# The second product of the last two blocks as seven products of half width

## The chip, the cores and the metric

The kernel runs on one core of a Trainium2 chip. A core has a matmul engine (PE; its weight loads are listed apart as PEld), a vector engine (VectorE, DVE in the profile), a scalar engine (ScalarE, ACT), GpSimd (POOL) and SyncE (SP); the last two issue transfers here, each on a queue of its own, and 16 transfer engines serve both. The metric is the device time of one execution in microseconds.

## The reference

A transformer block over 2048 tokens of 512 numbers: an adaptive layer norm (scale and shift from a condition row `c`), linear attention, a second adaptive layer norm, and a two-layer network with 1792 hidden columns. The change touches the last part only:

```python
h = layernorm(x) * (1 + cb) + sb
h = einsum("bsd,df->bsf", h, w1) + b1
act = mish(h)
x = x + gb * einsum("bsf,fd->bsd", act, w2)      # the second product
```

All of it is float32. D is 512, S is 2048, F is 1792.

## The kernel before

The tokens go in four blocks of 512, and the hidden columns in 14 tiles of 128 (`f`), or seven pairs of tiles (`g`). Every large product is made in "rounded" float32, whose matmul takes one pass: an operand is split into a high and a low half (`split`: ScalarE copies the high half, VectorE subtracts it for the low one), and `mm3` (lines 65 to 69) makes three matmuls, high by high, high by low and low by high. A matmul streams up to 512 columns past 128 x 128 weights, and each matmul loads its weights anew.

The first product takes two blocks together. `pair_unit(c0, g)` makes seven products instead of eight from 2 x 2 parts: two blocks of tokens by two halves of the 512 inputs by two tiles of w1 (a Strassen scheme; `rows(g)` makes the sums of w1's parts and splits them, `columns` those of the tokens). Each of the seven is six matmuls of 512 columns. VectorE adds the parts up from PSUM (`add`, line 848), ScalarE applies Mish (`mish`, `mish_b`). For the first of the two blocks the halves of the activations are made at once; those of the second wait in `ub` until `prep_a` splits them.

The second product is made block by block: `d_unit(b, f)` multiplies the four token tiles of tile `f` by w2's tile `f`, 512 columns, into four banks of PSUM (`oacc`), 12 matmuls; after the 14th tile VectorE adds the residual (line 831) and SP stores the block.

w2 is scaled by `gb` and split once (`w2_job`), and its halves are written to DRAM (`w2d`). They are used by block 0 at once; for blocks 1, 2 and 3 `w2_again` reads them back, 28 transfers of 256 KB a block on POOL's queue, four tiles ahead in block 1 and block 3. w1 is read and prepared by `rows` twice, once for blocks 0 and 1, once for 2 and 3.

The order of the work is written by hand: the engines' queues run in the order of the program. `spawn` puts a side job (a generator) on a list and `tick` takes each of them one step further, so that a step lands between two groups of matmuls. On-chip memory is 101 slots of 128 x 512 float32 (`sb`); a transfer into a slot waits for the last reader of what it held. The order from block 0 on is:

- for each pair `g`: `pair_unit(0, g)`, and, trailing by one or two tiles, block 0's `d_unit`; side jobs prepare w2 and the next w1, and the norms of blocks 2 and 3 (`norm_tile`).
- `second(1, prepare)`: block 1's 14 `d_unit`; side jobs transpose and prepare the tokens of blocks 2 and 3 and the first two w1 pairs again.
- for each pair: `pair_unit(2, g)`, trailed by block 2's `d_unit`.
- `second(3, end)`: block 3's 14 `d_unit`.

Of the kernel before, what the change touches and what calls it, by code (L numbers as in the profile page):

```python
# [8 lines left out]
F32 = mybir.dt.float32  # L9
F32R = mybir.dt.float32r  # L10
# [3 lines left out]
P = 128  # L14
# [11 lines left out]
def block_kernel(ctx: ExitStack, tc: tile.TileContext, x, wqkv, wo, w1, b1t, w2, c, wmodt, out):  # L26
# [23 lines left out]
    def spawn(gen):  # L50
        fresh.append(gen)

    def tick():

        running.extend(fresh)
        fresh.clear()
        for g in list(running):
            if next(g, "end") == "end":
                running.remove(g)

    def run(gen):
        for _ in gen:
            pass

    def mm3(o, st, mv, start, stop):

        pe.matmul(o, st[0], mv[0], start=start, stop=False)  # L67
        pe.matmul(o, st[0], mv[1], start=False, stop=False)  # L68
        pe.matmul(o, st[1], mv[0], start=False, stop=stop)  # L69

    def split(name, t, keep, key, lo_engine=dve, hi_engine=act):

        hi, lo = sb(f"{name}h", F32R, t.shape), sb(f"{name}l", F32R, t.shape)
        if hi_engine is act:
            act.activation(hi, t, AF.Copy)
        else:
            hi_engine.tensor_copy(hi, t)
        if lo_engine is dve:
            yield
        lo_engine.tensor_tensor(lo, t, f32(hi), op=ALU.subtract)  # L80
        keep[key] = hi, lo
# [412 lines left out]
            dve.tensor_scalar(zs[k], zbc, mc[:, k:k + 1], 1.0, op0=ALU.mult, op1=ALU.mult)  # L494


    w2s, w2d, op_a = {}, {}, {}

    w2r = {}

# [4 lines left out]
    def w2_job(f, wait=2):  # L505
        if f not in w2r:
            load_w2(f)
            for _ in range(wait):
                yield
        t = w2r[f]  # L510
        dve.tensor_tensor(t, t, bc["gb"], op=ALU.mult)
        yield
        yield from split(f"w2_{f}", t, w2s, f)
        yield
        for i in range(2):
            w2d[f, i] = drp.tile([P, D], F32R, name=f"w2d_{f}_{i}")
            pool.dma_start(w2d[f, i], w2s[f][i])

    def w2_again(f):

        w2s[f] = [sb(f"w2b_{f}_{i}", F32R) for i in range(2)]
        for i in range(2):
            pool.dma_start(w2s[f][i], w2d[f, i])  # L523

    def rows(g, wait):

        r = [sb(f"w1p_{g}_{i}", F32, (P, 4, P)) for i in range(2)]
        for i in range(2):
            f = 2 * g + i
            sp.dma_start(r[i], w1[:, P * f:P * (f + 1)].rearrange("(k p) f -> p k f", p=P))  # L530
        for _ in range(wait):
            yield
        a11, a12, a21, a22 = [r[i][:, 2 * k:2 * k + 2, :] for i in range(2) for k in range(2)]
        s12, s34 = [sb(f"s{n}_{g}", F32, (P, 4, P)) for n in (12, 34)]
        s1, s2, s3, s4 = s12[:, 0:2, :], s12[:, 2:4, :], s34[:, 0:2, :], s34[:, 2:4, :]
        dve.tensor_tensor(s1, a21, a22, op=ALU.add)
        dve.tensor_tensor(s2, s1, a11, op=ALU.subtract)
        dve.tensor_tensor(s3, a11, a21, op=ALU.subtract)
        dve.tensor_tensor(s4, a12, s2, op=ALU.subtract)
        yield  # L540
        keep, todo = {}, []
        for name, v, parts in (("a1", r[0], ("a11", "a12")), ("s12", s12, ("s1", "s2")), ("s34", s34, ("s3", "s4")),
                               ("a22", a22, ("a22",))):
            half = split(f"{name}_{g}", v, keep, name)
            next(half)
            todo.append((name, half, parts))
            if len(todo) == 2:
                yield
                for name, half, parts in todo:
                    run(half)  # L550
                    for i, part in enumerate(parts):
                        op_a[g, part] = [h[:, 2 * i:2 * i + 2, :] for h in keep[name]]
                todo = []

    early_rows = [rows(g, 1) for g in range(2)]

# [77 lines left out]
    def o_post(p, b, t):  # L634
        r = xt["r", b, t]
        dve.tensor_tensor(r, p, r, op=ALU.add)  # L636
        if b >= 2:
            yield
            d = x1d[b, t] = drp.tile([P, D], F32, name=f"x1d_{b}_{t}")
            pool.dma_start(d, r)  # L640

    def o_unit(b, t, tag="acc"):
        p = ps(tag, f"o_{b}_{t}")
# [50 lines left out]
    def load_back(key, src, b, t):  # L694
        v = xt[key, b, t] = sb(f"{key}b_{b}_{t}")
        sp.dma_start(v, src.pop((b, t)))
# [112 lines left out]
            tick()  # L809


    ag = {}

    def mish(p, b, f):
        u = sb(f"u_{b}_{f}")
# [5 lines left out]
    def d_unit(b, f):  # L821
        if f == 0:
            for t in range(4):
                oacc[t] = ps("acc", f"oacc_{b}_{t}")
        for t in range(4):
            ts = slice(P * t, P * (t + 1))
            mm3(oacc[t], [a[:, ts] for a in ag[b, f]], w2s[f], f == 0, f == NF - 1)
            if f == NF - 1:
                v = xt["r", b, t]
                r0 = 512 * b + P * t  # L830
                dve.tensor_tensor(v, oacc[t], v, op=ALU.add)  # L831
                sp.dma_start(out[r0:r0 + P, :], v)
# [61 lines left out]
    def ahead(b, u):  # L894

        if 0 <= u - NF + 4 < NF:
            w2_again(u - NF + 4)
        if 0 <= u - NF + 3 < NF:
            spawn(prep_a(b, u - NF + 3))

    G = NF // 2
    order = [(b, c + h) for c in range(2) for h in (0, 2) for b in (2, 3)]
# [1 line left out]
    def prepare(f):  # L904

        if f in (1, 3, 5, 7):
            for _ in range(2):
                transpose_f(*order.pop(0), "h")
        if f in (4, 8):
            spawn(columns(2, f // 4 - 1, ()))  # L910
        if f in (6, 10):
            spawn(rows((f - 6) // 4, 2))

    def end(f):
        if 4 <= f < 8:
            load_back("r", x1d, 3, f - 4)


    begun = {}
# [7 lines left out]
    def trail(f):  # L927
        if tiles:
            spawn(tiles.pop(0))
        d_unit(0, f)  # L930
        ahead(1, f)
        tick()

    for g in range(G + 1):
        if g < G:
            for f in (2 * g, 2 * g + 1) if g else ():
                spawn(w2_job(f))
            if g == 0:
                spawn(rows(2, 3))
            pair_unit(0, g, begun.pop(g, None))  # L940
            if 0 < g < G - 2:
                spawn(rows(g + 2, 2))
            if g == G - 1:
                for n in range(8):
                    load_back("n", nd, 2 + n // 4, n % 4)
        for f in ((0,), (1,))[g] if g < 2 else (2 * g - 2, 2 * g - 1):
            trail(f)
    second(1, prepare)
    for g in range(G + 1):
        if g < G:  # L950
            w2_again(2 * g)
            w2_again(2 * g + 1)
            pair_unit(2, g)
            if g + 2 < G:
                spawn(rows(g + 2, 2))
            if g == G - 2:
                for t in range(4):
                    load_back("r", x1d, 2, t)
        for f in (2 * g - 2, 2 * g - 1):
# [37 lines left out]
```

## Time and profile before

| | |
|---|---|
| median of 3 runs | 504.34 us (504.11 to 505.1) |
| profiled execution, its own time | 504.41 us |
| its span | 502.7 us |
| granted clock of the matmul engine | 1.00 |
| transfers | 77.29 MB, 60.83 MB read from DRAM, 15.99 MB written |

The profile is one execution. Its times are from the start of the span; the 1.7 us between the span and the time lie around it. In the timeline a row has the start, the length, the engine, the line of the kernel, the operation and the tiles (out<-in, buffer numbers left out), the partitions and elements, and the count where equal ones follow each other. In the table by stretches each engine has its busy time and its count of instructions, then come the granted clock, the mean busy share of the transfer engines and the rate. Matmuls overlap: the length of one holds its drain, and the step from one start to the next is what a matmul costs in a row of them.

### The profile page before, as it was taken

The page shows a single profiled execution, that of the slowest core. Times are in us where ns is not written, and L with a number is a line of the kernel's source. Part 1 is how long each engine was busy: PE and PEld are TensorE (multiplying, and loading weights), DVE is VectorE, ACT ScalarE, POOL GpSimd, SP SyncE. Part 2 cuts the span into 40 slices and gives each one's busy share as a digit, 9 for nine tenths or more (in the row PEclk, how much of TensorE's full clock was granted, in tenths as well). Part 3 has the DMA queues.
Part 4 walks back from the last instruction along what each step waited for, and adds up shares of the span by engine and source line. Part 5 has one row for each costly group of instructions (what it writes and reads, how often), then busy time and mean ns, then how long its engine had stood idle before and what let it go on. Part 6 is the DMA issues. An engine that isn't in the chain of part 4 may idle for free.

```text
span 502.7 us, 6896 instructions
## 1 busy us (share of the span) xinstructions
PE 495.2 (99%) x2396; PEld 405.5 (81%) x2396; DVE 360.1 (72%) x707; ACT 257.9 (51%) x463; POOL 113.7 (23%) x204
## 2 busy tenths in 40 slices
PE   7999999999999999999999999999999999999996
PEld 6778888878778888888888888888888888888885
DVE  6889785889997979987987776359885656745302
ACT  6766574523351978745777764366253355445000
POOL 4471000100212423000233345421110111470000
PEclk9999999999999999999999999999999999999999
DMA  8721503471554316352555498982941445596002
GB/s 310 277 83 44 166 22 106 145 254 53 141 131 135 84 43 193 106 167 65 185 172 188 152 316 257 349 237 74 261 134 45 124 126 157 154 359 221 31 1 83
DMA packets 52233, 77.29 MB, mean 154 GB/s; under 512 B 5805, under 2 KB 20277, under 8 KB 52198
## 3 DMA queue, kind: packets, MB, share of 16 engines
q0 software_dynamic: 19600, 37.45, 25.7%
q1 hardware_dynamic: 32452, 39.14, 24.9%
q8 instruction: 19, 0.31, 0.2%
q10 hardware_dynamic: 146, 0.26, 0.1%
q14 instruction: 16, 0.13, 0.1%
HBM read 60.83 MB, written 15.99 MB: 153 GB/s over the span
## 4 chain that ended last, share of the span: by engine, by line
PE 95%; DVE 2%; DMA 1%; ACT 1%; POOL 0%; issue 0%; ACTq 0%
PE oacc L67 10%; PE oacc L68 10%; PE oacc L69 10%; PE p_s L67 5%; PE p_s L68 5%; PE p_s L69 5%; PE p_a L67 4%; PE p_a L68 4%; PE p_a L69 4%; PE o L67 3%; PE pq L67 3%; PE o L69 3%; PE o L68 3%; PE pq L69 3%; PE pq L68 3%; PE gacc L68 3%
## 5 line engine op out<-in xcount | busy, mean ns | idle before, releaser
L523 POOL DMA_DIRECT2D w2b<-w2d x84 | 44.9, 538 | 101.7 <-PE p_a L69 27.3
L839 ACT ACTIVATE ub<-c,b1c 128x512 f32<-128x512 f32 x28 | 19.2, 719 | 57.0 <-DVE c L848 53.3
L848 DVE TENSOR_TENSOR u<-p_s,u 128x512 f32<-128x512 f32 x28 | 19.3, 691 | 35.2 <-PE p_s L69 25.6
L831 DVE TENSOR_TENSOR rb<-oacc,rb 128x512 f32<-128x512 f32 x8 | 5.5, 691 | 32.9 <-PE oacc L69 32.9
L848 DVE TENSOR_TENSOR u<-p_a,u 128x512 f32<-128x512 f32 x26 | 17.5, 687 | 7.6 <-PE p_a L69 6.9
L189 POOL TENSOR_TENSOR rs_n<-rs_n,half 128x1 f32<-128x1 f32 x16 | 9.8, 617 | 54.8 <-DVE rs_n L215 44.9
L705 ACT ACTIVATE hf_n<-tp_n,mc 128x512 f32<-128x512 f32 x16 | 11.7, 770 | 18.9 <-PE tp_n L703 18.9
L816 ACT ACTIVATE u<-u,b1c 128x512 f32<-128x512 f32 x26 | 18.5, 712 | 2.6 <-DVE u L848 2.6
L241 ACT ACTIVATE e_q<-pq 128x512 f32<-128x512 f32 x16 | 9.4, 588 | 20.0 <-PE pq L69 20.0
L848 DVE TENSOR_TENSOR c<-p_s,u 128x512 f32<-128x512 f32 x28 | 17.9, 681 | 2.3 <-PE p_s L69 2.3
L865 ACT ACTIVATE u<-p_a 128x512 f32<-128x512 f32 x12 | 7.1, 588 | 18.7 <-PE p_a L69 18.7
L241 ACT ACTIVATE e_k<-pk 128x512 f32<-128x512 f32 x16 | 9.4, 591 | 13.3 <-PE pk L69 13.1
L189 POOL TENSOR_TENSOR rs_x<-rs_x,half 128x1 f32<-128x1 f32 (+1 forms) x10 | 7.1, 716 | 33.0 <-DVE rs_x L184 32.2
L243 DVE TENSOR_SCALAR e_k<-e_k 128x512 f32<-128x512 f32 x16 | 6.8, 424 | 10.2 <-ACT e_k L241 10.0
L198 ACT ACTIVATE x<-x,nb_x,rs_x 128x512 f32<-128x512 f32 x15 | 11.5, 806 | 4.4 <-DVE nb_x L193 3.3
L624 DVE TENSOR_TENSOR q<-q,rd 128x512 f32<-128x512 f32 x16 | 10.5, 686 | 3.8 <-DMA rd<-rden_d 3.8
L612 POOL DMA_DIRECT2D rden_d<-rden x3 | 2.2, 738 | 43.4 <-DVE rden L610 43.4
L198 ACT ACTIVATE r<-r,nb_n,rs_n 128x512 f32<-128x512 f32 x8 | 6.5, 809 | 10.1 <-DVE nb_n L219 9.3
L244 DVE SCALAR_TENSOR_TENSOR ku<-pk,e_k 128x512 f32<-128x512 f32 x16 | 11.1, 692 | 0.7
L244 DVE SCALAR_TENSOR_TENSOR q<-pq,e_q 128x512 f32<-128x512 f32 x16 | 11.1, 691 | 0.7
L636 DVE TENSOR_TENSOR r<-o,r 128x512 f32<-128x512 f32 x16 | 10.8, 677 | 1.1 <-PE o L69 1.1
L180 DVE BATCH_NORM_STATS2 st_x<-x 128x6 f32<-128x512 f32 x13 | 8.9, 682 | 3.0 <-DMA x<-in_x_dram 3.0
(1118 smaller groups left out, 1751.5 us busy)
## 6 DMA issues: line engine op xcount, KB each, us to landing
w2b<-w2d POOLq DMA_DIRECT2D x84, 256.0 KB, 5.0
w1p<-in_w_dram SPq DMA_DIRECT2D x28, 256.0 KB, 3.5
wm<-in_wmodt_dram SPq DMA_DIRECT2D x24, 256.0 KB, 5.0
r<-in_x_dram SPq DMA_DIRECT2D x16, 256.0 KB, 2.7
x<-in_x_dram SPq DMA_DIRECT2D x15, 256.0 KB, 4.8
w2r<-in_w_dram SPq DMA_DIRECT2D x14, 256.0 KB, 2.7
rd<-rden_d POOLq DMA_DIRECT2D x12, 256.0 KB, 5.3
wr<-in_wqkv_dram SPq DMA_DIRECT2D x8, 256.0 KB, 4.8
```

The lines of the kernel that those rows point to most:

```text
L67: pe.matmul(o, st[0], mv[0], start=start, stop=False)
L68: pe.matmul(o, st[0], mv[1], start=False, stop=False)
L69: pe.matmul(o, st[1], mv[0], start=False, stop=stop)
L189: pool.tensor_tensor(y, y, half[:, lo:hi], op=ALU.pow)
L198: act.activation(dst, t, AF.Identity, bias=nb[key, b][:, j:j + 1], scale=rs[key, b][:, j:j + 1])
L241: act.activation(e, p, AF.Exp)
L244: dve.scalar_tensor_tensor(dst, p, 0.0, e, op0=ALU.max, op1=ALU.add)
L523: pool.dma_start(w2s[f][i], w2d[f, i])
L705: act.activation(hf[b, j], p, AF.Identity, bias=mc[:, 12 + j:13 + j], scale=mc[:, 16 + j:17 + j])
L816: act.activation(u, p, AF.Mish, bias=b1c[:, f:f + 1])
L839: act.activation(u, p, AF.Mish, bias=b1c[:, f:f + 1])
L848: dve.tensor_tensor(out, p, u, op=ALU.add)
```

## The change

Block 0 and the first product stay as they are. Five things change.

1. The second product of blocks 2 and 3 is made for both together, as seven products for each pair `g` (two blocks, two tiles of w2, two halves of 256 output columns). m1 and m2 use w2's parts as they are (`e_unit`, made between the `pair_unit`s), m4, m6, m7, m5 and m3 come after the last pair, each over all seven pairs. `seventh` makes one product for one pair: four token tiles, `mm3` on 256 columns, two token tiles to a bank.
2. The sums of w2's parts are made during block 1's second product (`w2_sums`), from the scaled w2, which `w2_job` now also writes to DRAM unsplit for pairs 0 to 4 (`w2f`), and are written to DRAM (`w2t`) for five of the pairs and kept for pairs 3 and 4. `load_wt` and `load_wb` read them and w2's own parts back.
3. The sums of the activations are made by `left_sums` and split, and `finish` adds the seven products up to the four quarters of the output, which are stored by quarter.
4. w1's operands, made once by `rows`, are written to DRAM for pairs 0 to 4 (`store_rows`, SP's queue) and read back for blocks 2 and 3 (`load_rows`, POOL's queue); those of pairs 5 and 6 stay in their slots, and the second round of pairs starts with them.
5. Block 1's second product takes the tiles of w2 in the order 10 to 13, 0 to 9, and the first four are still in their slots from block 0.

The core of it:

```diff
+    KEPT, SUMS_KEPT = 5, (3, 4)
 def w2_job(f, wait=2):
 ...
-            w2d[f, i] = drp.tile([P, D], F32R, name=f"w2d_{f}_{i}")
-            pool.dma_start(w2d[f, i], w2s[f][i])
+            pool.dma_start(w2d[g, i][:, n, :], w2s[f][i])
+        if g < KEPT:
+            pool.dma_start(w2f[g][:, n, :], t)
+    W2_AT = {0: 6, 1: 5, 2: 0, 3: 1, 6: 2, 10: 3, 12: 4}
+    def w2_sums(g):
+        if g < KEPT:
+            r = [sb(f"w2p_{g}_{i}") for i in range(2)]
+            for i in range(2):
+                sp.dma_start(r[i], w2f[g][:, i, :])
+        else:
+            r = [w2r[2 * g + i] for i in range(2)]
+        yield
+        yield
+        h = D // 2
+        b11, b12, b21, b22 = [v[:, c:c + h] for v in r for c in (0, h)]
+        ta, tb = [sb(f"t{n}_{g}") for n in (12, 34)]
+        t1, t2, t3, t4 = ta[:, 0:h], ta[:, h:D], tb[:, 0:h], tb[:, h:D]
+        for d, u, v in (t1, b12, b11), (t2, b22, t1), (t3, b22, b12), (t4, t2, b21):
+            dve.tensor_tensor(d, u, v, op=ALU.subtract)
+        yield
+        keep = {}
+        both = [split(f"t{i}_{g}", v, keep, i) for i, v in enumerate((ta, tb))]
 ...
+        d = w2t[g] = drp.tile([P, 2, 4, h], F32, name=f"w2t_{g}")
+        for i in range(2):
+            for n in range(2):
+                sp.dma_start(d[:, n, 2 * i:2 * i + 2, :], f32(keep[i][n]).rearrange("p (t c) -> p t c", t=2))
 ...
+    last_first = [*range(2 * KEPT, NF), *range(2 * KEPT)]
     def second(b, side):
-        for f in range(NF):
-            side(f)
-            ahead(b, f + NF)
+        for n, f in enumerate(last_first):
+            side(n)
+            ahead(b, n + NF)
             tick()
-            d_unit(b, f)
+            d_unit(b, f, n)
 ...
+    def seventh(name, tag, left, right, n, last):
+        if n == 0:
+            banks[name] = [ps(tag, f"{name}_{i}") for i in range(2)]
+        for t in range(4):
+            h = t % 2
+            mm3(banks[name][t // 2][:, D // 2 * h:D // 2 * (h + 1)], [a[:, P * t:P * (t + 1)] for a in left], right,
+                n == 0 and h == 0, n == last and h == 1)
+    def e_unit(n):
+        g = pairs[n]
+        for c, name in enumerate(("m1", "m2")):
+            seventh(name, "acc", ag[L, 2 * g + c], [w[:, c, :] for w in wb[g]], n, G - 1)
+    def left_sums(g):
+        a11, a12, a21, a22 = ua[2 * g], ua[2 * g + 1], ub[2 * g], ub[2 * g + 1]
+        yield from split(f"l4_{g}", a22, left, ("m4", g))
+        dve.tensor_tensor(a22, a21, a22, op=ALU.add)
+        dve.tensor_tensor(a21, a11, a21, op=ALU.subtract)
+        yield
+        dve.tensor_tensor(a11, a22, a11, op=ALU.subtract)
+        dve.tensor_tensor(a12, a12, a11, op=ALU.subtract)
 ...
-    for g in range(G + 1):
-        if g < G:
-            w2_again(2 * g)
-            w2_again(2 * g + 1)
-            pair_unit(2, g)
-            if g + 2 < G:
-                spawn(rows(g + 2, 2))
 ...
-            if f >= 0:
-                d_unit(2, f)
-            ahead(3, f)
-            tick()
-    second(3, end)
+    pairs = [5, 6, 0, 1, 2, 3, 4]
+    for n, g in enumerate(pairs):
+        if n < 5:
+            if n:
+                load_rows(n)
+            if n:
+                load_wb(pairs[n + 1])
 ...
+        pair_unit(L, g)
+        if n < 4:
+            spawn(left_trail(g))
+        if n:
+            e_unit(n - 1)
+            tick()
+    names = ["m4", "m6", "m7", "m5", "m3"]
+    units = [(name, n) for name in names for n in range(G)]
+    ahead_of = units[4:]
 ...
+    for k, (name, n) in enumerate(units[:4 * G]):
+        for _ in range(2 if k in (6, 10, 14, 18) else 1):
+            if ahead_of:
+                nm, m = ahead_of.pop(0)
+                spawn(left_prep(nm, pairs[m]))
 ...
+        seventh(name, tags[name], left.pop((name, pairs[n])), wt.pop((name, pairs[n])), n, G - 1)
+        if n == G - 1:
+            spawn(finish(name))
+        tick()
+        if k == 1:
+            e_unit(G - 1)
+            spawn(finish("m2"))
+            tick()
+    last = [ps("acc", f"m3_{t}") for t in range(4)]
+    for t in range(4):
+        p = last[t][:, 0:D // 2]
+        for n, g in enumerate(pairs):
+            mm3(p, [a[:, P * t:P * (t + 1)] for a in left["m3", g]], wt["m3", g], n == 0, n == G - 1)
+        tick()
+        v = rq[0, 1, t // 2][:, t % 2, :]
+        dve.tensor_tensor(v, v, p, op=ALU.add)
+        store(0, 1, t // 2, t % 2, t % 2 + 1)
```

`load_rows(0)` and the first two `load_wb` stand at the last two tiles of block 1's second product.

More of the change, by code (lines that the diff above doesn't have):

```diff
@@ L553, in rows, with store_rows, load_rows @@
                 todo = []
+    op_rows, rows_d = {}, {}
+    def store_rows(g):
+        for name, halves in op_rows.pop(g).items():
+            for i, h in enumerate(halves):
+                rows_d[g, name, i] = drp.tile(list(h.shape), F32, name=f"rd_{g}_{name}_{i}")
+                sp.dma_start(rows_d[g, name, i], f32(h))
+    def load_rows(g):
+        for name, parts in ("a1", ("a11", "a12")), ("s12", ("s1", "s2")), ("s34", ("s3", "s4")), ("a22", ("a22",)):
+            halves = []
+            for i in range(2):
+                d = rows_d.pop((g, name, i))
+                halves.append(sb(f"{name}b_{g}_{i}", F32R, d.shape))
+                pool.dma_start(halves[i], d)
+            for i, part in enumerate(parts):
+                op_a[g, part] = [h[:, 2 * i:2 * i + 2, :] for h in halves]
     early_rows = [rows(g, 1) for g in range(2)]
@@ L910, in prepare @@
             spawn(columns(2, f // 4 - 1, ()))
[L911 to L916, printed above, removed]
+        if f in W2_AT:
+            spawn(w2_sums(W2_AT[f]))
+        if f == NF - 2:
+            load_rows(0)
+            load_wb(5)
+        if f == NF - 1:
+            load_wb(6)
     begun = {}
@@ new lines, in left_trail, with left_prep, add_r, finish @@
+    def left_trail(g):
+        yield
+        yield
+        yield from left_sums(g)
+    def left_prep(name, g):
+        return left_sums(g) if name == "m4" else split(f"l_{name}_{g}", sums_of[g][name], left, (name, g))
+    def add_r(n, c, i, v, op=ALU.add):
+        dve.tensor_tensor(rq[n, c, i], rq[n, c, i], v, op=op)
+    def finish(name):
+        for i in range(2):
+            p = bank(name, i)
+            if name == "m2":
+                U[i] = sb(f"U_{i}", F32, (P, 2, D // 2))
+                act.activation(U[i], bank("m1", i), AF.Copy)
+                add_r(0, 0, i, bank("m1", i))
+                add_r(0, 0, i, p)
+                store(0, 0, i)
+            if name == "m4":
+                add_r(1, 0, i, p, ALU.subtract)
+            if name == "m6":
+                dve.tensor_tensor(U[i], U[i], p, op=ALU.add)
+                add_r(0, 1, i, U[i])
+            if name == "m7":
+                dve.tensor_tensor(U[i], U[i], p, op=ALU.add)
+                add_r(1, 0, i, U[i])
+                store(1, 0, i)
+                add_r(1, 1, i, U[i])
+            if name == "m5":
+                add_r(0, 1, i, p)
+                add_r(1, 1, i, p)
+                store(1, 1, i)
+            yield
@@ new lines, in block_kernel, with load_wt @@
+    wt, SUM = {}, {"m5": 0, "m6": 1, "m7": 2, "m4": 3}
+    def load_wt(name, g):
+        h = D // 2
+        if name != "m3" and g in SUMS_KEPT:
+            n = SUM[name]
+            wt[name, g] = [w2k[g][n // 2][i][:, h * (n % 2):h * (n % 2 + 1)] for i in range(2)]
+            return
+        v = sb(f"wt_{name}_{g}", F32R, (P, 2, h))
+        wt[name, g] = [v[:, i, :] for i in range(2)]
+        if name == "m3":
+            for i in range(2):
+                pool.dma_start(v[:, i, :], w2d[g, i][:, 1, D // 2:D])
+        else:
+            pool.dma_start(v, w2t[g][:, :, SUM[name], :])
@@ new lines, in block_kernel @@
+    units = [(name, n) for name in names for n in range(G)]
+    ahead_of = units[4:]
+    loads = list(units)
+    loads = loads[5:]
+    load_r(1, 0)
+    tags = {"m4": "h", "m6": "acc", "m7": "acc", "m5": "h"}
+    for k, (name, n) in enumerate(units[:4 * G]):
[3 more added lines that the diff above has]
+                spawn(left_prep(nm, pairs[m]))
+        for _ in range(2 if k < 3 else 1):
+            if loads:
+                nm, m = loads.pop(0)
+                load_wt(nm, pairs[m])
+        if k in (3, 8):
+            load_r(k // 8, 1)
+        seventh(name, tags[name], left.pop((name, pairs[n])), wt.pop((name, pairs[n])), n, G - 1)
[6 more added lines that the diff above has]
+            tick()
```

75 lines of the change are left out of this document (57 added, 18 removed).

## The prediction

> **What bounds the kernel now.** I read the page first: the busy shares, the chain that ended last, and the transfer rate by slice.
>
> ```profile
> span 502.7 us, 6896 instructions
> PE 495.2 (99%) x2396; PEld 405.5 (81%) x2396; DVE 360.1 (72%) x707; ACT 257.9 (51%) x463; POOL 113.7 (23%) x204
> GB/s 310 277 83 44 166 22 106 145 254 53 141 131 135 84 43 193 106 167 65 185 172 188 152 316 257 349 237 74 261 134 45 124 126 157 154 359 221 31 1 83
> PE 95%; DVE 2%; DMA 1%; ACT 1%; POOL 0%; issue 0%; ACTq 0%
> ```
>
> The matmul queue is busy for 99% of the span and makes 95% of the chain, and "issue" is 0%: time goes away only where matmul time goes away, and time is added only by a wait of the matmul queue. The best slice moved 359 GB/s, which I use as the transfer limit. Next, a table by stage: the first product of blocks 0 and 1 with block 0's second, block 1's second product, the two products of blocks 2 and 3, and block 3's second.
>
> ```profile
> core 0: us, PE busy (x) PEld busy (x) DVE busy (x) ACT busy (x) POOL busy (x), PEclk, DMA share, GB/s
> 230.00:314.00 84.00, 84.00 (x372) 69.56 (x371) 65.20 (x127) 57.14 (x109) 29.13 (x54) 1.00 0.66 199
> 314.00:355.60 41.60, 41.60 (x202) 34.76 (x201) 28.53 (x52) 21.42 (x38) 11.80 (x22) 1.00 0.75 219
> 355.60:460.20 104.60, 104.60 (x463) 86.63 (x462) 64.74 (x114) 48.78 (x85) 25.12 (x47) 1.00 0.58 167
> 460.20:498.40 38.20, 38.20 (x170) 31.39 (x168) 10.67 (x18) 0.00 (x0) 0.00 (x0) 1.00 0.16 57
> ```
>
> In all four PE is busy for the whole stretch at the full granted clock. VectorE has spare time everywhere (28.5 of 41.6 us is the tightest in which the change adds to it), the transfer engines are at 0.66 to 0.75 in the first two.
>
> **The price of a matmul of 512 columns.** The timeline of the matmul queue: the first and the last of block 3's 168 (14 tiles of w2, four output tiles, three passes).
>
> ```profile
> 460.28 0.39 PE L67 MATMUL oacc<-w2b,a_0h 128*128 128x512 f32 x1
> ...
> 498.13 0.39 PE L69 MATMUL oacc<-w2b,a_13l 128*128 128x512 f32 x1
> ```
>
> The 0.39 is the length of one with its drain; what counts is the step from start to start, (498.13 - 460.28) / 167 = 0.2266 us. Blocks 2 and 3 have 2 x 168 = 336 of them: 76.1 us, all on the path.
>
> **What they become.** Seven products for each of seven pairs of w2 tiles, four token tiles, three passes: 7 x 7 x 4 x 3 = 588 matmuls of 256 columns, each with a weight load of its own. They stream 588 x 256 = 150,528 columns where 336 x 512 = 172,032 were streamed. No matmul of 256 columns with these operands stands in the trace, so its step has to be bounded. At break-even it is 76.1 / 588 = 0.1295 us. Rows that bear on it, from the chain in order of time, the matmul timeline near the end, and the timeline of weight loads behind a group of transposes:
>
> ```profile
> 122.57 2.02 PE kv_ps L752 x64
> 132.99 3.43 PE m_ps L766 x8
> 496.55 0.39 PE L68 MATMUL oacc<-w2b,a_13h 128*128 128x512 f32 x1
> 496.55 0.19 PEld L69 LDWEIGHTS oacc<-w2b,a_13l 128*128 128x128 f32 x1
> 184.42 0.19 PEld L67 LDWEIGHTS o<-m_0h,qs_0h 128*128 128x128 f32 x1
> 184.53 0.19 PEld L68 LDWEIGHTS o<-m_0l,qs_0h 128*128 128x128 f32 x1
> 184.76 0.19 PEld L69 LDWEIGHTS o<-m_0h,qs_0l 128*128 128x128 f32 x1
> ```
>
> - Issuing is no limit: 64 small matmuls, each with its load, go in 2.02 us, 0.032 each.
> - Below: the next load starts with the matmul that runs (496.55 and 496.55). A load shows 0.19, but the second of two started 0.11 after the first (184.42, 184.53), so a load holds its path for 0.11 and the rest is latency. A step under 0.11 is excluded, for each matmul has a load.
> - If the step is all proportional to columns: half of 0.2266, 0.1133.
> - If a part of it is fixed: the eight plain f32 passes of 512 columns take 3.43 / 8 = 0.429 each. If they stream at half the rate of the rounded ones, 0.2145 of the 0.2266 is streaming and 0.0121 is not; 256 columns then take 0.1072 + 0.0121 = 0.119.
> - Above: if the whole 0.19 of a load were on the path, 0.19.
>
> I take 0.1195: it is nearest to the fixed part, since a swap of weights happens once a matmul whatever its width, and 0.11 and 0.1133 stay as the low end. 588 x 0.1195 = 70.3 us against 76.1: **5.8 us less**. The rule "TensorE: Matmul & The Clock Gate" in the Trainium skill, section "Back-to-back issue gap", has an isolated step of N/2.4 + 2.5 ns, 109 ns for 256; as an estimate from that page the sum would be 12 us less. The trace does not bear it out at 512 columns, where that formula gives 216 ns and the step is 227.
>
> **VectorE.** The added work falls in block 1's second product: seven `w2_sums`, each four subtractions of 256 columns and two low halves of 512; two `rows` jobs (four of 256, three of 512, one of 256) go. Steps between neighbours, from the VectorE timeline in that stage:
>
> ```profile
> 339.93 0.42 DVE L537 TENSOR_TENSOR s<-s,w1p 128x256 f32<-128x256 f32 x1
> 340.28 0.42 DVE L538 TENSOR_TENSOR s<-w1p,w1p 128x256 f32<-128x256 f32 x1
> ...
> 347.15 0.68 DVE L80 TENSOR_TENSOR t_1l<-t,t_1h 128x512 fp32r<-128x512 f32 x1
> 347.75 0.68 DVE L80 TENSOR_TENSOR a_12l<-ub,a_12h 128x512 fp32r<-128x512 f32 x1
> ```
>
> Back to back the steps are 0.35 and 0.60, less than the lengths. Added 7 x (4 x 0.35 + 2 x 0.60) = 18.2, removed 2 x (5 x 0.35 + 3 x 0.60) = 7.1: 28.5 + 11.1 = 39.6 of 41.6 us. It still fits, and the low halves that PE waits for (`prep_a`) are asked for three products, 3 x 12 x 0.2266 = 8.2 us, ahead. I put 0 to 1 us of waits here, 0.2 taken. ScalarE gets 14 high halves and loses 8: nothing.
>
> The other tight place is the turn from pairs to the products m4, m6, .... From the start of m4 to the first matmul of m6, PE has 84 matmuls of m4 and 24 of m1 and m2: 108 x 0.1195 = 12.9 us. VectorE has in that time three `left_sums` (four sums and a low half each), the four sums of `finish("m2")`, some two left of the last pair, and the first one for m6: 22 x 0.60 = 13.2 us. So 0 to 1.5 us of wait; I take 0.4. With a cheaper matmul this wait grows, at 0.1133 to 1.0, at 0.11 to 1.3. After that, `left_prep` is four units ahead of PE.
>
> **Transfers.** In the stretch 230 to 314 the change adds 10 x 0.26 MB of `w2f` and five times 1.8 MB of `store_rows`, 11.8 MB, to 199 x 84 = 16.7 MB: 28.5 MB, 339 GB/s, just under the 359. The stores stand on SP ahead of the later w1 and w2 loads, which are asked for a pair (15 us) ahead. In block 1's second product: ten `w2p` (2.6 MB), 20 `w2t` stores (5.2), eight of `load_rows(0)` (1.8), four `wb` (1.0) come; four `w1p` (1.0) and eight `w2b` (2.1, w2 tiles 10 to 13 are still in their slots) go. 219 x 41.6 = 9.1 MB becomes 16.6, 46 us at the best rate in a stretch of 41.6. The last 2.8 MB (rows and `wb`) are wanted two pairs later, two times 42 x 0.2266 = 19 us; what is wanted inside shares the engines with 13.8 MB, 38 us at 359. That hides, with little to spare:
>
> ```profile
> DMA to landing us min/median/max: 2.9/6.7/9.7
> ```
>
> This is w2b in the same stretch before. It is asked for four products, 10.9 us, ahead, so 1.2 us of cover stands over the worst. Afterwards the reads of blocks 2 and 3 are lighter than the 84 w2b were. "Kept weights" for block 1 itself gives nothing: PE does not wait at 314 in the table.
>
> **The end.** Four adds of 512 columns and four stores follow the last matmuls:
>
> ```profile
> 496.52 2.73 DVE L831 TENSOR_TENSOR rb<-oacc,rb 128x512 f32<-128x512 f32 x4 [27.53 <-PE oacc L69]
> ```
>
> After, the last add is of 256 columns, 0.42 for 0.68, and its store half as large: 0.3 less.
>
> Sum, against the profiled execution (504.41 us with a span of 502.7, 0.07 above the median of 504.34): 504.4 - 5.8 + 0.2 + 0.4 - 0.3 = **498.9 us**. No-change is within 0.2%, 1.0 us, about what a measurement can tell.
>
> **Rivals.**
> - *Columns or loads alone set the step.* At 0.1133 PE saves 9.5 us, at 0.11 11.4; with the wait at m6 0.6 or 0.9 us longer than counted, 495.8 or 494.2. For it: two loads 0.11 apart. Against: the 0.0121 above.
> - *The load is not hidden behind half as many columns.* Each matmul waits for its own load's 0.19: 588 x 0.19 = 111.7, 36 us more than now, 540. It decides from a step of 0.1295 on: 0.02 more than the 0.11 of a load would do. For it: PEld is 81% busy now and would have to run twice as often. Against: loads 0.11 apart, both of this form. In the Trainium skill, "TensorE: Matmul & The Clock Gate", section "Measured speedup vs the span model", a load overlaps running matmuls only where the row groups differ, which speaks against this change; by that rule every full-height matmul would pay for its load. The trace disagrees: the load at 496.55 starts with a full-height matmul and is over within its 0.2266.
> - *Transfers saturate in block 1's second product.* If the engines give 257 GB/s there, as in the slice between 316 and 349 in the transfer row, 13.8 MB take 53.7 us, 12.1 more than the stretch; less 1.2 of cover PE waits 10.9 us for w2b, or for low halves queued on VectorE behind a sum whose `w2p` has not come: 509.8. It turns the result from 285 GB/s down (13.8 MB in 41.6 + 1.2 + 5.6 us). For it: the two stretches at 339 and over. Against: 349 and 359 in single slices.
> - *The change doesn't do it.* Its instruction order has 252 more matmuls, 588 less 336; excluded.
>
> **How the numbers follow.** Forecast, 496.5 to 501.5: 0.50. Columns or loads alone: 0.22. Loads exposed: 0.10. Transfers: 0.15, of which a third ends under 503.4, about a fifth within 1 us. The rest, 0.03, slower through waits I have not seen. Faster 0.50 + 0.22 + 0.05 = 0.77, same 0.03, slower 0.20. The low end is the load's cadence, 494; the high end takes in most of the transfer rival, 508; outside are the exposed loads and little else.
>
> **What would show it.** The step of the matmuls of m4 to m3 in the matmul timeline: 0.12 is the forecast, 0.113 and under the first rival, 0.13 and more the second. PE's idle time before L69 of block 1's oacc, w2b landings over 10.9 us, and DMA share near 1 in that stretch would show the third. A wait of PE for VectorE at m6 of 0.4 us would confirm the turn. The forecast is wrong if PE has idle time over 3 us in all, or if the step lies outside 0.110 to 0.1295.

## The result, and the profile after

The changed kernel takes **499.4 us** (median of four runs, 499.22 to 499.57) where the kernel before takes 504.28 (four runs, 504.11 to 505.1): a ratio of 0.99, 95% interval 0.9883 to 0.9917. The forecast was 498.9, the range 494 to 508. The profiled execution of the changed kernel took 499.34 us with a span of 497.6.

The page of the changed kernel: the span, the busy shares, the rate by slice and the chain that ended last.

```profile
span 497.6 us, 7730 instructions
PE 490.2 (98%) x2648; PEld 412.9 (83%) x2648; DVE 394.6 (79%) x758; ACT 265.2 (53%) x472; POOL 136.8 (27%) x238
GB/s 298 295 84 44 157 33 107 129 275 43 142 139 129 96 30 251 92 366 270 239 344 312 227 278 201 335 321 383 377 343 221 66 173 86 218 189 243 91 43 86
PE 79%; issue 11%; POOL 4%; DVE 3%; DMA 1%; ACT 1%; POOLq 0%; DVEq 0%; ACTq 0%
```

There are 252 more matmuls and 5 us less of busy PE. The chain of waits has changed its look: 11% "issue" and 7% VectorE and GpSimd, where before PE held 95% of it. That is no idle time of PE, as the table by stretches shows. The first two stretches are those of the table before; then come the pairs of blocks 2 and 3, the end of the pairs with the turn to m4, and the products from there on.

```profile
core 0: us, PE busy (x) PEld busy (x) DVE busy (x) ACT busy (x) POOL busy (x), PEclk, DMA share, GB/s
230.00:314.00 84.00, 84.00 (x373) 69.54 (x372) 65.23 (x128) 57.01 (x109) 29.69 (x55) 1.00 0.82 265
314.00:355.60 41.60, 41.60 (x199) 34.29 (x198) 36.52 (x70) 24.71 (x44) 14.60 (x27) 1.00 1.11 362
355.60:420.00 64.40, 64.40 (x330) 55.24 (x329) 50.13 (x80) 26.58 (x43) 22.82 (x40) 1.00 0.73 202
420.00:443.00 23.00, 23.00 (x138) 20.52 (x138) 13.74 (x22) 9.91 (x15) 10.48 (x15) 1.00 0.78 195
443.00:496.00 53.00, 50.56 (x420) 50.15 (x418) 38.53 (x63) 16.41 (x31) 10.93 (x19) 1.00 0.43 120
```

PE is busy all the time up to 443, at the full granted clock. (The last stretch reaches 1.8 us past the last matmul.) The chain runs through other engines in stretches in which PE did not idle, so the table decides here. The two stretches in which the transfers were expected to be dear moved 265 and 362 GB/s (the best slice of the page 383, where before it was 359); a busy share of 1.11 says that packets overlap on one engine.

The matmul timeline of the changed kernel, in m4 and at the turn to m6:

```profile
450.07 0.28 PE L68 MATMUL m<-t_3l,l_3h 128*128 128x256 f32 x1
...
452.95 0.28 PE L68 MATMUL m<-wt_m,l_m_5h 128*128 128x256 f32 x1
453.87 0.39 PE L69 MATMUL m<-wt_m,l_m_5l 128*128 128x256 f32 x1 [0.64 <-DVE l_m_5l L80]
454.09 0.28 PE L67 MATMUL m<-wt_m,l_m_5h 128*128 128x256 f32 x1
```

From 450.07 to 452.95 lie 24 steps: 0.120 each. Over the whole timeline, 579 of the 587 steps of this kind lie between 0.115 and 0.125. The row at 453.87 is the largest single wait in the changed part: 0.92 from start to start instead of 0.12, so 0.80 us lost, of which 0.64 shows as idle (the matmul ahead still drains in the rest). The step behind the wait is long too, 0.22 from 453.87 to 454.09, another 0.10: the wait costs 0.90 in all.

The other places where PE lost time, from the same timeline: block 1's second product, and the turn from 256 columns back to 512 at the start of a pair.

```profile
350.36 0.39 PE L68 MATMUL oacc<-w2b,a_8h 128*128 128x512 f32 x1
350.73 0.50 PE L69 MATMUL oacc<-w2b,a_8l 128*128 128x512 f32 x1
351.07 0.39 PE L67 MATMUL oacc<-w2b,a_8h 128*128 128x512 f32 x1
...
377.77 0.40 PE L67 MATMUL p_a<-b_0h,a1b 128*128 128x512 f32 x1
...
379.16 0.39 PE L67 MATMUL p_s<-t_0h,s12b 128*128 128x512 f32 x1
```

Two steps of 0.37 and 0.34 for 0.227 at 350.36 and 350.73, with another of 0.33 three microseconds earlier, make 0.36 us. The six steps from 377.77 to 379.16 take 1.39 for 1.36: 0.03 us lost behind each of five such turns, 0.14 in all. At the six turns the other way the first step of 256 columns takes 0.113, so 0.04 comes back.

What VectorE did at the two waits, from its timeline in the changed kernel:

```profile
349.99 0.69 DVE L80 TENSOR_TENSOR a_8l<-ub,a_8h 128x512 fp32r<-128x512 f32 x1
...
439.95 0.68 DVE L80 TENSOR_TENSOR l_2l<-ub,l_2h 128x512 fp32r<-128x512 f32 x1
...
442.12 0.69 DVE L1066 TENSOR_TENSOR u<-ub,u 128x512 f32<-128x512 f32 x1
442.85 0.69 DVE L1067 TENSOR_TENSOR u<-u,u 128x512 f32<-128x512 f32 x1
443.46 0.68 DVE L80 TENSOR_TENSOR l_3l<-ub,l_3h 128x512 fp32r<-128x512 f32 x1
...
453.13 0.68 DVE L80 TENSOR_TENSOR l_m_5l<-u,l_m_5h 128x512 fp32r<-128x512 f32 x1
```

The low half `a_8l` ends at 350.68 and the matmul that reads it starts at 350.73; `l_m_5l` ends at 453.81 and its matmul starts at 453.87. In both cases PE waits for the low half that has just been made. The rows from 442.12 to 443.46 show why VectorE was slower at the turn than the forecast had it: the sum at 442.85 (line 1067) reads the result of the one at 442.12 (line 1066) and follows after 0.73, when that one has ended, while the low half `l_3l`, which has nothing to do with the sum before it, follows after 0.61. The other sums of a pair don't all read the result of the one before them, but they overwrite a tile which that one reads, and their steps are 0.72 or 0.73 too. From 439.95 to the end of `l_m_5l` at 453.81 stand 20 instructions in 13.86 us, 0.69 each.

The stage starts, in the kernel before and then in the changed one, and the end of the changed one:

```profile
355.56 0.39 PE L67 MATMUL p_a<-b_0h,a_0h 128*128 128x512 f32 x1
```

```profile
355.86 0.39 PE L67 MATMUL p_a<-b_0h,a_5h 128*128 128x512 f32 x1
...
493.92 0.28 PE L69 MATMUL m<-wt_m,l_m_4l 128*128 128x256 f32 x1
494.24 0.42 DVE L1177 TENSOR_TENSOR rq<-rq,m 128x256 f32<-128x256 f32 x1 [2.10 <-PE m L69]
494.69 0.33 SPq L1039 DMA_DIRECT2D out_dram<-rq  x1
```

**The account.** From the first matmul of the pairs to the last matmul before took 498.13 - 355.56 = 142.57 us and after 493.92 - 355.86 = 138.06: 4.51 less. The last matmul's own step is not in these, so 587 x 0.12 = 70.44 stand there for 335 x 0.2267 = 75.94 (5.50 less), the wait at m6 with the step behind it (+0.90) and the turns of width (0.14 - 0.04, +0.10): 4.50 less. The stage starts 0.30 later. From the last matmul's start to the end of the span was 4.53 and is 3.71 (0.82 less). In all -4.51 + 0.30 - 0.82 = -5.03, against 504.41 - 499.34 = 5.07.

### The profile page after: what moved, and what is told of

Its sections match the earlier page's. It is cut to its first block, busy times and chain, and to the rows that moved or that the text cites. A ratio compares the mean times of both kernels' runs of the same rounds, so it can differ in the third digit from the quotient of the medians.

```text
span 497.6 us, 7730 instructions
## 1 busy us (share of the span) xinstructions
PE 490.2 (98%) x2648; PEld 412.9 (83%) x2648; DVE 394.6 (79%) x758; ACT 265.2 (53%) x472; POOL 136.8 (27%) x238
## 4 chain that ended last, share of the span: by engine, by line
PE 79%; issue 11%; POOL 4%; DVE 3%; DMA 1%; ACT 1%; POOLq 0%; DVEq 0%; ACTq 0%
PE oacc L69 5%; PE oacc L68 5%; PE oacc L67 5%; PE p_s L69 3%; PE p_s L68 3%; PE p_s L67 3%; PE o L67 3%; PE pq L67 3%; PE o L69 3%; PE o L68 3%; PE pq L69 3%; PE pq L68 3%; PE m L69 3%; PE m L68 3%; PE m L67 3%
## 5 line engine op out<-in xcount | busy, mean ns | idle before, releaser
L1122 POOL DMA_DIRECT2D wt_m<-w2t x20 | 14.0, 702 | 23.3 <-PE p_s L69 15.1
L241 ACT ACTIVATE e_k<-pk 128x512 f32<-128x512 f32 x16 | 9.3, 590 | 13.2 <-PE pk L69 12.9
L573 POOL DMA_DIRECT2D w2b<-w2d x20 | 10.7, 538 | 18.4 <-DMA out_dram<-r 5.3
L567 POOL DMA_DIRECT2D wb<-w2d x14 | 9.9, 710 | 13.1 <-PE p_a L69 9.6
```

Of the source, the lines that this page charges most:

```text
L241: act.activation(e, p, AF.Exp)
L1122: pool.dma_start(v, w2t[g][:, :, SUM[name], :])
```

## The experiments

The theory: a matmul costs a fixed 12 ns and its columns, and in a row of them no less than the 0.11 of a weight load on average; what else was lost are two places where VectorE's order is late; and the transfers just hide. Seven kernels put that against its rivals.

**Widths and weights, each by itself.** In the kernel before, block 3's matmuls are cut to 256 + 256, 384 + 128 and 320 + 192 columns for three tiles each, and for two tiles take only 64 of the 128 weight columns. The cuts tell a fixed part (0.0121) from a step in proportion to columns, and show what a load costs under a matmul of 128 columns, which streams too short to hide it.

```diff
 def d_unit(b, f):
-            mm3(oacc[t], [a[:, ts] for a in ag[b, f]], w2s[f], f == 0, f == NF - 1)
+            if b < NB - 1 or f in (0, 12, 13):
+                mm3(oacc[t], [a[:, ts] for a in ag[b, f]], w2s[f], f == 0, f == NF - 1)
+            elif f < 10:
+                cut = (256, 256, 256, 256, 384, 384, 384, 320, 320, 320)[f]
+                for lo, hi in (0, cut), (cut, D):
+                    mm3(oacc[t][:, lo:hi], [a[:, ts] for a in ag[b, f]], [w[:, lo:hi] for w in w2s[f]], False, False)
+            else:
+                mm3(oacc[t][0:64, :], [a[:, P * t:P * t + 64] for a in ag[b, f]], w2s[f], False, False)
```

> The kernel before, with block 3's second product cut into other widths: tiles 1 to 3 of w2 as 256 + 256 columns, 4 to 6 as 384 + 128, 7 to 9 as 320 + 192, tiles 10 and 11 with weights of 64 columns instead of 128 past 512 columns (the other half of the tokens is left out of these two tiles). Theory 1, a part of the step is fixed: from 0.2266 at 512 and 0.120 at 256 the step is 0.0134 + 0.000416 N, so 0.173 at 384 and 0.147 at 320; for 192 and 128 this gives 0.093 and 0.067, and the load that starts with the matmul before holds its path for 0.11, so both come out at 0.11 (the first theory without a floor: 0.093 and 0.067). Rival, the load is hidden only while it is much shorter than the matmul: 320 and 384 in line, but 192 and 128 at 0.19. With 64 columns of weights: 0.2266 if the fixed part is the swap, 0.220 if it is the load taking turns with the stream, for then half the load costs half. The time: 36 matmuls at 256 instead of 18 at 512 cost little each way; in all 3 to 6 us more than the kernel before.

The matmul timeline of this kernel, the first matmul of each stretch, and then two weight loads under matmuls of 128 columns:

```profile
463.55 0.28 PE L67 MATMUL oacc<-w2b,a_1h 128*128 128x256 f32 x1
...
472.18 0.34 PE L67 MATMUL oacc<-w2b,a_4h 128*128 128x384 f32 x1
...
482.49 0.36 PE L67 MATMUL oacc<-w2b,a_7h 128*128 128x320 f32 x1
...
491.81 0.39 PE L67 MATMUL oacc<-w2b,a_10h 128*64 128x512 f32 x1
...
497.33 0.39 PE L67 MATMUL oacc<-w2b,a_12h 128*128 128x512 f32 x1
```

```profile
472.71 0.19 PEld L68 LDWEIGHTS oacc<-w2b,a_4h 128*128 128x128 f32 x1
472.82 0.19 PEld L69 LDWEIGHTS oacc<-w2b,a_4l 128*128 128x128 f32 x1
```

The steps: (472.18 - 463.55) / 72 = 0.1199 at 256; 10.31 / 36 = 0.2864 for a pair of 384 and 128; 9.32 / 36 = 0.2589 for 320 and 192; 5.52 / 24 = 0.2300 with 64 weight columns. With the fixed 0.0121 and 0.000419 a column, 384 costs 0.173 and 320 costs 0.146; that leaves 0.113 for 128 columns and 0.113 for 192, so a floor of about 0.11 is there for both, and nothing like 0.19. It is the cadence of the loads, which start 0.11 apart there (472.71, 472.82). The floor holds for the mean of a row: the starts of single matmuls lie unevenly, 0.06 to 0.11 apart behind 128 columns and 0.17 to 0.23 behind 384. By columns alone a pair would have been 0.2266, with the fixed part but no floor 0.239. The whole took 508.95 us in a single run, 4.5 more than before; from the steps it should be 3.9. The half load did not shorten the step (0.230, where the steps of whole loads in this run have a mean of 0.227), so the fixed part does not go by the length of the load; what it is stays open.

**One more trail of sums (the wait at m6).** In the changed kernel `left_sums` trails the pairs for five pairs, not four, so that one pair's sums (a low half and four sums) fall out of the turn.

```diff
-        if n < 4:
+        if n < 5:
             spawn(left_trail(g))
 ...
-    ahead_of = units[4:]
+    ahead_of = units[5:]
```

> The changed kernel with the activation sums of one more pair (the fifth) made during the pairs, ahead of m4. Theory: the wait of PE at the start of m6 (0.64 us in the profile, a step of 0.92 for 0.12) is VectorE's 13 us of work against PE's 13 us there; taking 3 us of it away ends the wait, 0.8 us less, 498.6. Rival: the wait moves on to the next product or into the pairs, and the time is the same within 0.2 us.

Measured: 498.52 us (498.48 to 498.57), ratio to the kernel before 0.9885, interval 0.9869 to 0.9902; 0.9 less than the changed kernel. The same place in its matmul timeline:

```profile
453.07 0.28 PE L68 MATMUL m<-wt_m,l_m_5h 128*128 128x256 f32 x1
453.19 0.28 PE L69 MATMUL m<-wt_m,l_m_5l 128*128 128x256 f32 x1
```

The step is 0.12 again, and the time went by the 0.90 that the wait and the step behind it had cost. The wait was VectorE's order and nothing else.

**Block 1 reads all its weights again.** Here block 1 takes its tiles in the order 0 to 13 and reads all 14 back. It adds 2.1 MB of reads close to the stretch that already moves 362 GB/s, and asks whether the kept tiles bring anything.

```diff
-    last_first = [*range(2 * KEPT, NF), *range(2 * KEPT)]
+    last_first = [*range(NF)]
 ...
-        if 0 <= u - NF + 4 < NF and last_first[u - NF + 4] < 2 * KEPT:
+        if 0 <= u - NF + 4 < NF:
```

> The changed kernel with block 1 taking w2's tiles in the order 0 to 13, all 14 read back (part 5 of the change undone): 2.1 MB more into block 1's second product, where the profile after shows 362 GB/s and the engines taken for the whole stretch. Theory, that the kept weights themselves give nothing: the same within 0.5 us, since the reads are asked for four products ahead and what is added is late only for rows wanted two pairs later. Rival, that at a full transfer share each byte counts: 2.1 MB at 362 GB/s is 5.8 us of engine time, and PE waits for w2b up to that, 3 to 6 us slower.

Measured: 499.6 us (499.39 to 500.0), ratio 0.9908, interval 0.9893 to 0.9922, not to be told from the changed kernel. Block 1's second product in its table by stretches:

```profile
314.00:355.60 41.60, 41.44 (x198) 33.99 (x197) 36.02 (x70) 24.23 (x43) 14.14 (x26) 1.00 1.10 356
```

PE lost 0.16 us there, and the rate did not rise. But the reads are asked for four products ahead, and seven of the eight that came on top were issued before 314 (15 of `w2b` between 296 and 314, for 8 in the changed kernel); from 236.4 to 314 the rate rose from 265 to 286 GB/s. So kept weights are worth nothing to the time, as the theory has it; what 2.1 MB more inside the full stretch would cost, this run does not show.

**w1's operands prepared again.** Now part 4 of the change is undone: no `store_rows`, no `load_rows`, and VectorE and ScalarE make the operands a second time, as before.

```diff
-            load_rows(0)
+            spawn(rows(0, 2))
 ...
-            if g < G - 2:
-                store_rows(g)
 ...
-                load_rows(n)
+                spawn(rows(n, 2))
```

> The changed kernel with w1's operands of pairs 0 to 4 made again by the rows job instead of written and read back (part 4 undone): 18 MB of transfers less, 3.55 us of VectorE more for each of five pairs, 18 us in a stretch of 88 in which VectorE is busy for 64. Theory, PE waits only where VectorE has no room: the first pair's job falls into block 1's second product, where VectorE is busy for 36.5 of 41.6 and reaches 40, and the pairs get 14 us into 24 spare: 0.5 to 2.5 us slower. Rival, transfers are what strains the new kernel: with 18 MB less it is 0.4 to 1 us faster.

Measured: 503.73 us (503.57 to 503.91), ratio 0.9988, interval 0.9979 to 0.9997: 4.3 more than the changed kernel. The direction was expected, the size was not. From its table by stretches, the pairs; from its matmul timeline the two largest waits, with two rows behind the second; and from its VectorE and ScalarE timelines what was ahead of the instructions that PE waited for:

```profile
355.60:420.00 64.40, 62.08 (x315) 51.91 (x314) 59.06 (x107) 33.05 (x59) 5.59 (x8) 1.00 0.39 103
```

```profile
366.29 0.50 PE L67 MATMUL p_a<-b_0h,a_6h 128*128 128x512 f32 x1 [0.68 <-DVE c L918]
...
373.66 0.50 PE L67 MATMUL p_s<-b_0h,s_6h 128*128 128x512 f32 x1 [1.63 <-ACT u L935]
374.00 0.40 PE L68 MATMUL p_s<-b_0l,s_6h 128*128 128x512 f32 x1
374.24 0.39 PE L69 MATMUL p_s<-b_0h,s_6l 128*128 128x512 f32 x1
```

```profile
363.49 0.42 DVE L586 TENSOR_TENSOR s<-w1p 128x256 f32<-128x256 f32 x1
...
364.95 1.28 DVE L918 TENSOR_TENSOR c<-p_s,u 128x512 f32<-128x512 f32 x2
...
370.18 0.40 ACT L75 ACTIVATE a_0h<-w1p 128x256 fp32r<-128x256 f32 x1
```

VectorE has 59.1 us of work in 64.4 where the changed kernel has 50.1. By the sums that still fits; but the waits are for `add` (`c`) and Mish (`u`) of the pair itself, and these are queued behind pieces of the jobs. From 362.02 to 364.95 VectorE makes four subtractions of the last of w2's sums and then four of `rows` (363.49 is the first), and `add` starts at 364.95 where it started at 363.41 in the changed kernel. ScalarE then makes four high halves of `rows` (370.18 is the last) ahead of Mish, whose copy (line 935) starts at 373.03 for 369.63; VectorE has nothing to do from 370.7 until it comes. Both waits come before the first `e_unit`, so they are no matter of its being shorter than `d_unit`. From the first matmul of the pairs to the last of the kernel it took 141.75 us for the changed kernel's 138.06, 3.7 more, of which about 3.0 lies in these two waits and the steps behind them. The other 0.6 lies after the last store's issue (3.54 for 2.94 us), for which no run shows a cause. So undoing part 4 gives back 4.3 of the 4.9 us that the whole change brought: in this order of the jobs, the seven products by themselves would have been paid for with waits for VectorE and ScalarE.

**Every store of w2's sums made twice.** 20 more stores of 256 KB on SP's queue in block 1's second product, with nothing that reads them. It measures how much cover the transfers still have there.

```diff
                 sp.dma_start(d[:, n, 2 * i:2 * i + 2, :], f32(keep[i][n]).rearrange("p (t c) -> p t c", t=2))
+                sp.dma_start(drp.tile([P, D], F32, name=f"w2x_{g}_{i}_{n}"), f32(keep[i][n]))
```

> The changed kernel with each store of w2's sums issued twice on SP's queue, the second time into DRAM that nobody reads: 20 transfers, 5.2 MB, 14.5 us of the 16 engines at the 362 GB/s that the stretch 314 to 355.6 now shows. It measures the cover that is left for transfers there. Theory A, that w1's rows and wb, wanted 13 us later, take up the lateness: 0 to 2 us slower. Theory B, that loads of the unsplit w2 on the same queue come late, VectorE stands behind their subtractions, and the low halves and PSUM behind VectorE: 8 to 15 us slower, with PE waiting for VectorE and not for a transfer.

Measured: 512.91 us in a single run, 13.5 more than the changed kernel. From its waits, its table by stretches (block 1's second product, and two stretches inside the first wait) and its matmul timeline:

```profile
DVE t L545 <- DMA w2p<-w2f: 13.2, 6, 3.8
```

```profile
314.00:355.60 41.60, 38.27 (x173) 31.41 (x172) 32.07 (x61) 23.70 (x42) 12.04 (x22) 0.92 1.10 381
345.10:347.60 2.50, 0.00 (x0) 0.00 (x0) 1.41 (x4) 0.52 (x1) 0.00 (x0) 1.00 1.13 390
347.70:348.30 0.60, 0.00 (x0) 0.00 (x0) 0.60 (x3) 0.51 (x2) 0.00 (x0) 0.50 1.06 410
```

```profile
344.65 0.39 PE L68 MATMUL oacc<-w2b,a_6h 128*128 128x512 f32 x1
348.37 0.80 PE L69 MATMUL oacc<-w2b,a_6l 128*128 128x512 f32 x1 [3.33 <-DVE a_6l L80]
348.96 0.63 PE L67 MATMUL oacc<-w2b,a_6h 128*128 128x512 f32 x1
349.39 0.63 PE L68 MATMUL oacc<-w2b,a_6h 128*128 128x512 f32 x1
...
376.74 0.80 PE L67 MATMUL p_a<-b_0h,a_6h 128*128 128x512 f32 x1 [5.18 <-DVE c L919]
```

VectorE waits 13.2 us for `w2p`, which stands on SP's queue behind stores; PE then waits for a low half, and later for an `add`, queued behind the sums on VectorE. That is the path which the prediction's transfer rival named. A `w2p` takes hardly longer to land than in the changed kernel (8.8 to 9.2 us for 8.2 to 8.9), but the loads that VectorE waited for ahead of PE's two waits were issued 3.1 and 14.1 us later (337.09 for 334.03, 364.03 for 349.93): it is their place behind the stores that makes them late. The stretch moved 381 GB/s, hardly more than the 362 of the changed kernel, so 5.2 MB more do not fit, and somewhere within them lies the point at which this rival decides. Of the 13.5 us, the two waits make 3.5 and 5.35 beyond a normal step. About 5 more come from the clock: after each of the two waits the steps are 0.43 (348.96, 349.39) for some 14 and 12 matmuls, twice the 0.227.

**The low halves asked for one product earlier (the waits in block 1).**

```diff
-        if 0 <= u - NF + 3 < NF:
-            spawn(prep_a(b, last_first[u - NF + 3]))
+        if 0 <= u - NF + 4 < NF:
+            spawn(prep_a(b, last_first[u - NF + 4]))
```

> The changed kernel with the activations of blocks 1 split four products ahead instead of three. The profile after has three steps of 0.33 to 0.37 for 0.227 at 347 to 351, 0.36 us over in all, where VectorE runs through 24 operations of 512 columns without a pause. Theory, VectorE's order there: they go, 0.3 to 0.4 us less, 499.0. Rival, w2b or its queue: nothing changes, for transfers are asked for as before.

Measured: 498.77 us (498.66 to 498.96), ratio 0.9891, interval 0.9874 to 0.9907; 0.6 less than the changed kernel, a little more than was expected. Its matmul timeline at the place of the late low half:

```profile
350.15 0.39 PE L68 MATMUL oacc<-w2b,a_8h 128*128 128x512 f32 x1
350.38 0.39 PE L69 MATMUL oacc<-w2b,a_8l 128*128 128x512 f32 x1
```

The step is 0.23; the wait for `a_8l` is gone.

**Both.** The two edits that each take a wait away, the longer trail of sums and the earlier low halves, together:

> The fifth pair's activation sums early and the split four products ahead, both. If the two waits are independent, the gains add up: 499.4 - 0.9 - 0.35 = 498.15, PE without a wait from 210 us to the end. If VectorE's work is only shifted, no better than the better of the two, 498.5.

Measured: **498.18 us** (498.11 to 498.38), ratio 0.988, interval 0.9865 to 0.9894. That is what was expected of two independent waits (498.15), and better than either edit alone; the gains measured singly, 0.9 and 0.6, come to 0.3 more than the 1.2 here, about the spread of the runs. This version beats both kernels, by 6.1 and 1.2 us. No wait of PE is listed after 210 us; what is left of the time in blocks 2 and 3 is matmul steps.

## Why the prediction held, step by step

- **The step of 256 columns.** Taken 0.1195 between 0.11 and 0.1133 below and 0.19 above; measured 0.120, so between the first start and the last 5.50 us less for 5.8 (0.11 more for the last matmul's own step, which is counted at the end). The rivals on either side fall by the same row, and by the kernel of cut widths: 0.1199 at 256, and the load's floor at 0.11, as a mean, shown where the columns are too few. The reading that carried it was the weight loads' cadence (0.11) against their shown length (0.19), and the fixed part worked out of two matmuls of different speed. The Trainium skill's rule that a load overlaps only between row groups, which spoke against the change, does not hold for this form of matmul: 0.120 a step with a full-height load for each. (In "TensorE: Matmul & The Clock Gate" the rule stands in the section "The mechanism", not in the one that the prediction names; the same section also has a load pulled ahead when it goes to a background buffer of weights, which the prediction left out and which does not speak against the change.)
- **VectorE in block 1.** Taken 39.6 of 41.6 us and 0.2 of waits; measured 36.5 and 0.36. The last of w2's sums slid past the end of the stretch (four subtractions and four low halves stand after 355.6, 3.8 us by the forecast's steps), which is why it holds less. The waits are inside the 0 to 1 given.
- **The turn to m6.** Taken 0.4 (0 to 1.5); measured 0.80, and 0.10 in the step behind it. The place was right, and the experiment that takes one pair's sums out got it back whole. The term was mis-sized because all 22 steps of VectorE were priced at 0.60, the step of neighbours that don't depend on each other. Most of the sums depend on the one before and step at 0.72: 20 instructions took 13.9 us where 22 were put at 13.2, against PE's 108 x 0.12 = 13.0.
- **The end.** Taken -0.3; measured -0.82, the largest error. Only the add's own 0.27 was counted (0.42 for 0.69). The last matmul drains 0.11 sooner, and the half-size last store takes 2.94 us from its issue to the end of the span where the whole one took 3.38 (from 499.28), 0.44 less. That this goes by its size is not shown: the same half-size store took 2.94 in five kernels, but 3.54 in the one that prepares w1's operands again and 2.67 in the one with doubled stores.
- **Turns of width.** Not foreseen: 0.10 us in all.
- **Transfers.** The stretch was put at 16.6 MB, 359 GB/s and "little to spare"; it moved 362 GB/s and every w2b landed inside the 10.9 us ahead of it:

```profile
DMA to landing us min/median/max: 3.8/5.6/8.1
```

  This is w2b in 314 to 355.6 of the changed kernel. The rival did not come true at this load. The doubled stores show that it would have at 5.2 MB more, by the path that it named. The stretch ahead was put at 339 GB/s and moved 265, 6.2 MB less: from 211 to 230 us, ahead of it, the changed kernel moves 330 GB/s where the one before moves 118, which is 4.0 MB of them, and seven reads of the kept tiles, 1.8 MB, were issued before 314 in the kernel before and go from there, not from block 1's stretch.
- **Kept weights nothing.** Held: the kernel that reads all of block 1's weights again takes the same time.
- **What the sum did not price.** Taking `rows` out of the pairs was booked only in block 1's stretch. Its part in the pairs, 3.7 us there when undone, stood nowhere, since before the change PE hid it (VectorE had 64.7 of 104.6 us there). The change takes the job out, so the forecast was not hurt by this; that is luck and not foresight, for with the seven products alone, in this order of the jobs, the same sum would have been wrong by about 4 us.

So -5.50 + 0.36 + 0.90 + 0.10 - 0.82 = -5.0 stands against the forecast's -5.8 + 0.2 + 0.4 - 0.3 = -5.5. The end came out 0.5 better than forecast and the turn 0.5 worse: these two errors cancel, and that the total lies so near the forecast is luck in this part.

## What to carry to other kernels

Price a narrower matmul by its step from start to start, as a fixed part and a part by columns, with the cadence of the weight loads as the floor; the lengths of rows tell neither. When side jobs move, ask what then stands ahead, in each engine's queue, of the instructions that PE waits for: a sum over the stage said that VectorE had 5 us to spare, and the matmuls still lost 3.7. Where a low half or a sum is made just before its use, asking for it one step earlier takes a line or two and gave 1.2 us here for two places.

## What the runs showed of the hardware that was not expected

In the kernel with the doubled stores, PE's clock fell to half in each of its two long waits, and stayed there after the matmuls had begun again. The granted clock is 1.00 from 345.1 to 347.6, inside the first wait, and 0.50 from 347.7 on; after the waits of 3.33 and 5.18 us the steps were 0.43 for 14 and some 12 matmuls, about 5 us beside 8.8 of waits. After the wait of 1.63 us in the kernel that prepares w1's operands again, only the next step is longer (0.34 from 373.66 to 374.00, then 0.24), with a granted clock of 1.00. From which length between 1.63 and 3.33 us on a wait has this cost, no run here shows. The Trainium skill's "TensorE: Matmul & The Clock Gate", section "What's actually happening", has the rate halved after an idle window of about 3.4 us; the trace agrees with the halving, and has the clock down within 2.7 us of the end of the last matmul before the first wait (345.04). Four further points: a VectorE instruction of 512 columns that reads the result of the one before it, or overwrites what that one reads, steps at 0.72, others at 0.60; a load of 64 weight columns does not make a matmul's step shorter (0.230 for 0.227 in the same run); packets overlap on the transfer engines, whose share reached 1.11 at 362 GB/s; and 381 GB/s was the most that a 40 us stretch of reads and writes moved.
